# A re-annealed instruction order for an adaLN attention and GEGLU block on one core: refitted transfer model, loads moved by first use, clock-keeping matmuls redistributed

## The chip, the cores and the metric

The kernel runs on one core of one Trainium2 chip. The metric is the device time of one execution in microseconds (us), as timed from outside. The profile's span of the core is shorter by nearly a constant: the two differ by 1.7 to 1.9 us. A run more than 1.5% above the fastest of its kernel is called slow and left out of ratios.

Engines: PE is TensorE, DVE is VectorE, ACT is ScalarE, POOL is GpSimd, SP is SyncE, which here only issues DMAs. All large loads share one queue: queue q1 moved 28.56 of the 28.84 MB (part 3 of the page), and SP's timeline has the loads in the order of the program.

## The reference, cut to what matters

```python
mod = silu(c) @ w_mod                        # six vectors of 512: sa, ca, ga, sb, cb, gb
h = layernorm(x) * (1 + ca) + sa             # x is 2048 x 512, bf16
q, k, v = split(h @ wqkv)                    # 32 heads of 16
# each position looks at 8 earlier ones, two apart (dilated, local)
o = softmax(q . k[pos - 2*w] * scale) @ v[pos - 2*w]
x = x + ga * (o @ wo)
h = layernorm(x) * (1 + cb) + sb
x = x + gb * ((gelu(h @ w_gate) * (h @ w_up)) @ w_down)    # 512 -> 1792 -> 512
```

## The kernel before

The kernel cuts the 2048 rows into five groups (256, 256, 512, 512, 512) and pipelines them: QKV and the attention of one group run beside the feed-forward part (FFN) of the group before. It does not issue instructions as it goes. Every piece of work is recorded as an operation with an estimated duration; 948 of them are then emitted in the order that a list, `ORDER`, gives. That list came from an annealing search over a small time model, which is part of the kernel's source. The model decides one thing at build time too: how many clock-keeping matmuls (matmuls on zeros, whose result nobody reads) are put in front of a TensorE operation.

```python
ORDER = [0, 8, 52, 1, 6, 38, 28, 5, 29, 30, ...]      # 948 indices, cut

class Plan:
    LAND = 1.65
    SLOW = (4.0, 1.7)         # assumed in the model: the transfer pipe stands still for 1.7 us after 4.0 us
    # ...
    def emit(self):
        placed = self.order()
        pes, early = [o for o in placed if o.eng == "pe"], True
        for o, q in zip(pes, pes[1:]):
            early = early and o is not self.cold
            q.fill = int((q.at - o.at - o.us - 0.2) / 0.216) if early else 0
        # ... then emits each operation, with q.fill clock-keeping matmuls ahead of it
```

`self.cold` is one clock-keeping matmul that stands between the last transposes of the first group and its QKV; after it none is added. (The transposes of the second group, eight of them, may stand in between too.) These are the loads that the argument touches. They are numbered in the order in which they are recorded, not in which they are issued:

```python
load_x(0, 2, -1000)                                   # op 6: rows of the first group (x0)
load_cols(wm01, w_mod, 0, 2 * D, -999)                # op 7: sa, ca
first = [load_cols(wq, A_wqkv, 0, D, -998)]           # op 8: Q weights
load_x(2, 4, -997, first)                             # op 9: rows of the second group (x1)
load_cols(wkv, A_wqkv, D, 3 * D, -996)                # op 10: K and V weights
load_x(4, 8, -989, first)                             # op 11: rows of the third
# ...
for i in range(2):
    load_cols(Wg[i], B_w_gate, i * F // 2, (i + 1) * F // 2, -894 + 2 * i)
    load_cols(Wu[i], B_w_up, i * F // 2, (i + 1) * F // 2, -893 + 2 * i)
# ...
for i in range(2):                                    # the two halves of w_down
    lo, hi = i * FT // 2, (i + 1) * FT // 2
    dma(918e3, ..., out=WdP[:, lo:hi, :], ...)        # WdP0, WdP1
```

An FFN of the first group needs all of Wg and Wu; this kernel takes the second column halves (Wg1, Wu1) first, so the last gate and up weights to be loaded are Wg0 and Wu0. "The second half of Wu" in the prediction means the one loaded second, which is Wu0.

## Time and profile before

| what | where it is read | before |
|---|---|---|
| time, median of 3 runs (range) | timer | 254.38 us (253.68 to 254.77) |
| span of the profiled run | head of the page | 251.0 us |
| TensorE busy | page, part 1 | 240.7 us, 96% |
| half clock | clock record | 13.20 to 16.61 us |
| longest wait of TensorE | waits | 2.4 us, for Wu |
| clock-keeping matmuls, the first 14 of warm-up included | built program | 28 |

Part 1 of the page of the kernel before, with the span above it (busy time, share, number of instructions):

```profile
span 251.0 us, 4233 instructions
...
PE 240.7 (96%) x1624; PEld 126.4 (50%) x1642; DVE 165.9 (66%) x313; ACT 151.5 (60%) x278; POOL 18.0 (7%) x43
```

TensorE is busy nearly all the time, so a new order can only win the little that is not busy, and what runs at half clock. The waits of TensorE, before (what waited, for what: us in total, times, the longest):

```profile
PE u_ps L745 <- DMA Wu<-in_B_w_up_dram: 2.4, 1, 2.4
PE warm_ps L401 <- DVE neghalf L289: 1.3, 1, 1.3
PE tp L507 <- DVE xn L483: 1.0, 1, 1.0
...
PE g_ps L745 <- DMA Wg<-in_B_w_gate_dram: 0.3, 1, 0.3
```

The longest one is for a weight half that is in the queue behind others. SP's timeline, before, shows the order of issue (start, us to issue, line, what; the landing is elsewhere in the trace, Wu at 65.6 us):

```profile
52.53 0.64 SPq L391 DMA_DIRECT2D WdP<-in_B_w_down_dram  x1
...
56.61 0.60 SPq L365 DMA_DIRECT2D Wu<-in_B_w_up_dram  x1
...
57.93 0.60 SPq L391 DMA_DIRECT2D WdP<-in_B_w_down_dram  x1
```

So half of the down weights (0.9 MB) goes ahead of the up weights that TensorE will need first. The other place is the start. The windows view, before (stretch, its length, busy time and count of PE, PEld, DVE, ACT and POOL, then the share of full TensorE clock, the DMA share and GB/s):

```profile
7.00:12.00 5.00, 4.47 (x57) 2.49 (x55) 3.27 (x11) 0.96 (x5) 4.03 (x12) 1.00 1.06 386
12.00:16.00 4.00, 3.27 (x19) 2.42 (x21) 3.74 (x11) 2.71 (x7) 2.39 (x11) 0.65 1.08 317
...
60.00:75.00 15.00, 12.55 (x106) 7.59 (x105) 10.31 (x17) 9.89 (x18) 0.00 (x0) 1.00 1.11 254
```

TensorE's clock is halved over most of 12 to 16 us, when QKV of the first group starts; and in 60 to 75 us TensorE is busy for only 12.55 of 15 us, at full clock. No other stretch of the 250 us has as much to win.

### The profile page before, as it was taken

How to read it: one execution, taken by the hardware profiler on the slowest of the kernel's cores; microseconds unless marked ns; L12 is line 12 of the kernel's file. 1: busy time of each engine (PE TensorE's matmuls, PEld its weight loads, DVE VectorE, ACT ScalarE, POOL GpSimd, SP SyncE). 2: the span in 40 equal slices, each digit the busy share in tenths (PEclk: the TensorE clock that was granted, in tenths of full speed). 3: DMA queues.
4: the chain of work that ended last, by engine and by line, in shares of the span. 5: the costliest groups of instructions: out<-in, count | busy, mean ns of one | idle time of the engine just before them, and what ended most of it. 6: DMA issues, size and time to landing. Idle time of an engine off the chain costs nothing.

```text
span 251.0 us, 4233 instructions
## 1 busy us (share of the span) xinstructions
PE 240.7 (96%) x1624; PEld 126.4 (50%) x1642; DVE 165.9 (66%) x313; ACT 151.5 (60%) x278; POOL 18.0 (7%) x43
## 2 busy tenths in 40 slices
PE   7899999989699999999999999999999999999993
PEld 2489655556447575655444444444444444444441
DVE  1799999999578999879999555765345413122213
ACT  2258879689389955696463778506549821657300
POOL 1740220200001000010000010000001100000000
PEclk9979999999999999999999999999999999999999
DMA  6995999999994430554330006601000402000001
GB/s 178 376 310 149 212 274 264 275 296 334 278 204 112 89 83 1 138 123 104 109 64 0 3 19 129 129 24 61 0 3 0 84 0 81 6 0 0 0 24 63
DMA packets 36566, 28.84 MB, mean 115 GB/s; under 512 B 12865, under 2 KB 34626, under 8 KB 36546
## 3 DMA queue, kind: packets, MB, share of 16 engines
q1 hardware_dynamic: 36544, 28.56, 45.6%
q8 instruction: 13, 0.21, 0.4%
q14 instruction: 7, 0.06, 0.1%
q10 hardware_dynamic: 2, 0.00, 0.0%
HBM read 21.40 MB, written 4.28 MB: 102 GB/s over the span
## 4 chain that ended last, share of the span: by engine, by line
PE 87%; DMA 5%; DVE 3%; ACT 1%; issue 1%; POOL 1%; SPq 1%; POOLq 0%
PE y_ps L767 19%; PE u_ps L745 19%; PE g_ps L745 19%; PE qkv_ps L558 16%; PE x_ps L722 5%; DMA Wu<-in_B_w_up_dram 4%; PE o_ps L707 3%; PE LT L614 3%; DMA x_sg<-in_A_x_dram 2%; DVE st L473 1%; PE LT L645 1%; PE tp L507 1%; PE mb_ps L444 1%; PE rB L676 1%; ACT vT L563 1%
## 5 line engine op out<-in xcount | busy, mean ns | idle before, releaser
L745 PE MATMUL u_ps<-h2T,Wu 128*128 128x512 bf16 (+1 forms) x280 | 55.6, 337 | 2.4 <-DMA Wu<-in_B_w_up_dram 2.4
L745 PE MATMUL g_ps<-h2T,Wg 128*128 128x512 bf16 (+1 forms) x280 | 55.3, 337 | 0.3 <-DMA Wg<-in_B_w_gate_dram 0.3
L767 PE MATMUL y_ps<-WdP,hht 128*128 128x512 bf16 x217 | 49.5, 379 | 0.4
L756 ACT CAST ub<-u_ps 128x512 bf16<-128x512 f32 x56 | 32.3, 589 | 23.5 <-PE u_ps L745 22.8
L754 ACT ACTIVATE gl<-g_ps 128x512 bf16<-128x512 f32 x56 | 32.9, 601 | 21.5 <-PE g_ps L745 21.1
L757 DVE TENSOR_TENSOR hht<-gl,ub 128x512 bf16<-128x512 bf16 x56 | 23.0, 422 | 34.5 <-ACT gl L754 18.7
L745 PEld LDWEIGHTS <-Wu 128*128 128x128 bf16 x280 | 26.9, 98 | 25.8 <-DMA Wu<-in_B_w_up_dram 2.9
L745 PEld LDWEIGHTS <-Wg 128*128 128x128 bf16 x280 | 26.7, 98 | 24.3 <-issue 2.5
L767 PEld LDWEIGHTS <-hht 128*128 128x128 bf16 x224 | 21.7, 98 | 25.6
L558 PE MATMUL qkv_ps<-hT,wkv 128*128 128x512 bf16 (+1 forms) x157 | 31.2, 337 | 0.2
L598 DVE TENSOR_TENSOR pq<-qT,kT 128x2048 bf16<-128x2048 bf16 x24 | 28.1, 1219 | 0.1
L691 DVE TENSOR_TENSOR pv<-e,vR 128x2048 bf16<-128x2048 bf16 x24 | 28.0, 1218 | 0.1
L479 POOL TENSOR_TENSOR rstd<-rstd,neghalf 128x2 f32<-128x2 f32 x16 | 12.7, 794 | 176.2 <-DVE rstd L468 111.3
L774 DVE TENSOR_TENSOR ot<-y_ps,x_sg 128x512 bf16<-128x512 f32 x16 | 11.0, 691 | 20.9 <-PE y_ps L767 20.1
L558 PEld LDWEIGHTS <-wkv 128*128 128x128 bf16 x160 | 17.1, 114 | 8.4 <-issue 1.1
L558 PE MATMUL qkv_ps<-hT,wq 128*128 128x512 bf16 (+1 forms) x79 | 17.1, 362 | 0.1
L722 PE MATMUL x_ps<-woP,oT 128*128 128x512 bf16 x58 | 15.0, 379 | 0.3
L713 ACT CAST oT<-o_ps 128x512 bf16<-128x512 f32 x16 | 9.0, 592 | 9.8 <-PE o_ps L707 9.8
L473 DVE BATCH_NORM_STATS2 st<-x_sg 128x6 f32<-128x512 bf16 x16 | 10.8, 675 | 4.3 <-DMA x_sg<-in_A_x_dram 4.3
L495 ACT ACTIVATE h2T<-h2T,modT,scl 128x512 bf16<-128x512 bf16 (+1 forms) x16 | 11.0, 751 | 4.0 <-DMA h2T<-xn 4.0
L465 ACT ACTIVATE xn<-x_sg,xsum 128x512 bf16<-128x512 bf16 x16 | 11.5, 718 | 3.2 <-DVE xsum L462 3.0
L726 DVE SCALAR_TENSOR_TENSOR x_sg<-x_ps,x_sg 128x512 bf16<-128x512 f32 x16 | 10.7, 686 | 3.2 <-PE x_ps L722 3.2
(88 smaller groups left out, 214.0 us busy)
## 6 DMA issues: line engine op xcount, KB each, us to landing
vR<-scr SPq DMA_DIRECT2D x24, 260.0 KB, 4.5
vR<-scr SPq DMA_DIRECT2D x8, 264.0 KB, 6.9
wm<-in_w_mod_dram SPq DMA_DIRECT2D x4, 512.0 KB, 5.3
out_dram<-ot SPq DMA_DIRECT2D x16, 128.0 KB, 1.7
Wg<-in_B_w_gate_dram SPq DMA_DIRECT2D x2, 896.0 KB, 6.0
Wu<-in_B_w_up_dram SPq DMA_DIRECT2D x2, 896.0 KB, 9.4
WdP<-in_B_w_down_dram SPq DMA_DIRECT2D x2, 896.0 KB, 6.8
scr<-vT SPq DMA_DIRECT2D x6, 264.0 KB, 4.7
```

The costliest lines, as they stand in the source:

```text
L465: act(0.75, lambda i=i, xn=xn, nm=nm, mv=mv, c0=c0: nc.scalar.activation(out=xn[:, i, :], in_=x[g, c0 + i], func=ACT.Square, bias=nm[:, i: ...
L473: dve(0.59, lambda i=i, st=st, c0=c0: nc.vector.bn_stats(out=st[:, i, :], in_=x[g, c0 + i]), r=[x.key(g, c0 + i)], w=[(st, i)], pri=p)
L479: gp(0.65, lambda rstd=rstd: nc.gpsimd.tensor_tensor(out=rstd[:], in0=rstd[:], in1=neghalf[:, 0:2], op=ALU.pow), r=[rstd, neghalf], w=[rst ...
L558: nc.tensor.matmul(ps[:, j - j0, :], lhsT=(wkv[:, dt, (b - 1) * D + j:b * D:4] if b else wq[:, dt, j:D:4]), rhs=h_cols(hT, g, dt), start=( ...
L598: dve(1.14, lambda j=j, wg=wg, t=pq[m]: nc.vector.tensor_tensor(out=t[:], in0=_ap(q[g][:, j, 0:n], [[0, 4], [1, n]]), in1=_ap(k[g][:, j, : ...
L691: dve(1.14, lambda jj=jj, jl=jl, wg=wg, t=pv[m]: nc.vector.tensor_tensor(out=t[:], in0=_ap(e[:, wg, :], [[0, 4], [1, n]]), in1=vR[g][jj][: ...
L722: nc.tensor.matmul(x1_ps[:], lhsT=oT[:, j, c4 * P:(c4 + 1) * P], rhs=woP[:, j, :], start=(j == 0), stop=(j == 3))
L745: nc.tensor.matmul(ps[:, ft - f0, :], lhsT=Wt[ft // 7][:, dt, ft % 7 * P:(ft % 7 + 1) * P], rhs=h_cols(h2, g, dt), start=(dt == 0), stop=( ...
L754: act(0.485, lambda gl=gl, ps=gu[0]: nc.scalar.activation(out=gl[:], in_=ps[:], func=ACT.Gelu_apprx_tanh), r=[gu[0]], w=[gl], pri=p, table ...
L756: act(0.475, lambda ub=ub, ps=gu[1]: nc.scalar.copy(out=ub[:], in_=ps[:]), r=[gu[1]], w=[ub], pri=p)
L757: dve(0.335, lambda gl=gl, ub=ub, ht=ht: nc.vector.tensor_tensor(out=ht[:], in0=gl[:], in1=ub[:], op=ALU.mult), r=[gl, ub], w=[ht], pri=p)
L767: nc.tensor.matmul(y_ps[:], lhsT=hh[ft // nf][:, ft % nf, c4 * P:(c4 + 1) * P], rhs=WdP[:, ft, :], start=(ft == 0), stop=(ft == FT - 1))
```

## The change: intent and diff

The same arithmetic is emitted in another order. The order was annealed again over a model whose constants had been refitted: slower transfers, later landings, shorter VectorE operations in the softmax, up to about 1 us of extra slack (`late`) for weights. The clock-keeping rule was made slightly more generous, and the last one before QKV is asked to carry two more.

```diff
 ORDER = [
-    0, 8, 52, 1, 6, 38, 28, 5, 29, 30, 39, 36, 37, 40, 41, 43, 9, 130, 4, 42, 31, 7, 11, 33, 32, 44, 131, 34, 10, 35,
+    5, 52, 51, 0, 29, 28, 6, 36, 37, 9, 38, 128, 129, 1, 30, 39, 40, 41, 42, 43, 44, 47, 130, 131, 7, 132, 32, 31, 11,
     ... (948 indices, nearly all moved; cut)
-    SLOW = (4.0, 1.7)
+    SLOW = (4.0, 1.5)
     ... (model of drain latency on VectorE and TensorE; cut)
-            q.fill = int((q.at - o.at - o.us - 0.2) / 0.216) if early else 0
+            q.fill = max(q.warm, int((q.at - o.at - o.us - 0.1) / 0.216)) if early else 0
-        self.dma = lambda n, fn, bw=360e3, ring="sp", **kw: ...
+        self.dma = lambda n, fn, bw=350e3, ring="sp", **kw: ...
     def load_wm(b, p, after=()):
-            late=0.3 if b > 1 else 0.0)
+            bw=330e3, late=1.0)
-    first = [load_cols(wq, A_wqkv, 0, D, -998)]
+    load_cols(wq, A_wqkv, 0, D, -998)
-                pl.cold = pe(0.22, filler, r=[warm, tp], w=[wps], pri=-960)
+                pl.cold = pe(0.66, filler, r=[warm, tp, modT, scl], w=[wps], pri=-960)
+                pl.cold.warm = 2
-                    r=[scr], w=[(t, r)], pri=-985 if g == 0 else -950, bw=205e3, late=0.3)
+                    r=[scr], w=[(t, r)], pri=-985 if g == 0 else -950, bw=185e3, late=0.7)
```

What comes out, from building both: the clock-keeping matmuls fall from 28 (14 of warm-up, 13 ahead of the modulation columns, 1 among the transposes) to 17 (14 of warm-up, and 3 between the modulation columns and the second group's transposes, after which QKV starts). The loads at the start become x0, x1, wm01, x of the third group, wkv, wq, where they had been wq, x0, x1, wm01, x of the third group, wkv; QKV of the first group begins with K and V. Later, Wu0 is issued ahead of both halves of WdP instead of between them.

## The prediction

> **What bounds the kernel now.** TensorE. The page has it busy 240.7 of 251.0 us (96%), VectorE 165.9, ScalarE 151.5; the chain of waits is 87% TensorE. In the timeline I compared each matmul's start-to-start time with the pace of its shape (about 0.216 us for 512 columns). From 75 us to the last matmul at 247 us almost nothing is lost, so a new order gains nothing there. What can be won is small and early:
>
> 1. Start. The first QKV matmul starts at 13.73 us, after clock-keeping matmuls, modulation columns and transposes; the last transposes waited 1.04 us for xn.
> 2. Clock. The trace has TensorE at half clock for 3.4 us, from 13.2 to 16.6 us, just as QKV begins (windows view: 0.81 granted over 14 to 21 us, 1.00 later). That costs about 1.7 us.[...]
> 3. Weights. At 62.8 us TensorE waits 2.4 us[...] for the second half of Wu, whose load stands in the DMA queue behind half of WdP. It is TensorE's longest wait.
> 4. Two waits near 51 and 55 us (modulation columns, Wg), about 1 us together.
> 5. The tail, 247.0 to 251.0 us: output add 0.69 us, store 1.7 us. Unchanged.
>
> **What the change does.** No arithmetic changes; work is reordered. Building both: 28 clock-keeping matmuls become 17, so "more" holds only for the three (was one) just before QKV. That removes 11 x 0.216 us, but in time that waits for data: worth nothing by itself. Loads start with x, not wq, and wq comes after wkv; QKV of the first group starts with K and V. In the trace 3.67 MB stood up to the end of wkv, which landed at 14.3 us; now 3.15 MB, at about 0.36 MB/us: about 12.9 us (estimate). x lands at about 4.1 instead of 5.5 us, wm01 at 8.7 instead of 10.1, so LN and modulation are no longer last: QKV starts at 12.9 us, bound by wkv, 0.8 us sooner. V to scratch starts near 15.5 us instead of 21.25, closing the hole in DMA at 20 to 24 us. The second half of Wu is issued before both halves of WdP, 0.9 MB sooner, and lands before its use. Item 3 goes.
>
> **Sum.** Start -0.8, Wu -2.5, small waits -0.5; clock -1.7 with chance 0.35 only, because TensorE now idles 1 to 2 us before wkv lands, with 0.65 us of clock-keeping work in that window: -0.6 on average. New small stalls +0.4. Net -4.0 us: 250.4 us. All of it is on the critical path: TensorE is saturated from there to the end, so what is won before 70 us passes through.
>
> **Chances.** 250.4 us, range 248.6 to 252.4. Faster by over 2% (under 249.3): 0.27; within 2%: 0.71; slower: 0.02.
>
> **What the profile would show.** First QKV matmul at 12.5 to 13.2 us, released by the DMA of wkv; no TensorE wait over 0.5 us for Wu; the first logits fold at 21 to 23 us (24.86 now); last matmul to end still 3.9 us. A half-clock window of about 3.4 us still near 13 us in the likelier case; if gone, I am 1.2 us too high.
>
> **What would make it wrong.** wkv landing after 13.5 us[...]; two half-clock windows instead of one; vR gathers ahead of hT transposes starving QKV of group 3 near 45 to 60 us; Wu still late because the queue is blocked behind a gather that waits for VectorE.

The sum came to -4.0 us (-0.8 - 2.5 - 0.5 - 0.6 + 0.4), from 254.38 to 250.4 us. The rate of 0.36 MB/us agrees with the windows view of the kernel before (355 GB/s from 3 to 14 us). The 1.7 us of the clock term are half of the 3.41 us at half clock in that trace; its chance of 0.35, and that idling ahead of QKV brings the half clock, were the author's estimate, which e3, e4 and e9 test.

## More of the kernel before

The down weights are scaled by `gb` in place on VectorE, in seven pieces of two slices:

```python
for f0 in range(0, FT, 2):
    dve(0.6, ... out=WdP[:, f0:f0 + 2, :], in0=WdP[:, f0:f0 + 2, :], in1=gbB ...)   # ops 79 to 85
```

Slices 0 to 6 come with the load WdP0, slices 7 to 13 with WdP1.

## The result, and the profile after

Ratios are the mean time of one kernel's fast runs over that of the other kernel's fast runs of the same rounds, so they are not quite the ratio of the medians quoted. The kernel after took **250.62 us (median of 4, 250.25 to 251.22)** against 254.06 us (253.68 to 254.77) for the one before in the same rounds: ratio **0.9864, 95% interval 0.983 to 0.9897**, so within 2%. The profiled spans are 251.0 and 248.5 us, a difference of 2.5 us, against 3.4 us for the medians; the point "Medians and spans" near the end comes back to that.

Part 1 of the page, after:

```profile
span 248.5 us, 4223 instructions
...
PE 237.8 (96%) x1613; PEld 125.0 (50%) x1631; DVE 166.1 (67%) x313; ACT 153.3 (62%) x278; POOL 18.6 (7%) x43
```

The waits of TensorE, after. The wait for Wu is gone and none over 0.8 us is left on weights; the 2.1 us at the top lies in the warm-up, where nothing is lost by it:

```profile
PE c_ps L422 <- DMA crow<-in_c_dram: 2.1, 1, 2.1
PE tp L515 <- DVE xn L491: 1.7, 2, 1.1
PE modT_ps L437 <- DMA wm<-in_w_mod_dram: 0.8, 1, 0.8
PE mb_ps L452 <- DMA wm<-in_w_mod_dram: 0.4, 1, 0.4
PE qkv_ps L567 <- DMA wkv<-in_A_wqkv_dram: 0.3, 1, 0.3
```

SP's timeline, after. Wu is issued 4.4 us sooner, before both halves of WdP; it landed at 58.8 us and was first used at 59.67:

```profile
52.26 0.64 SPq L373 DMA_DIRECT2D Wu<-in_B_w_up_dram  x1
53.00 1.37 SPq L579 DMA_DIRECT2D scr<-vT  x2
54.41 1.53 SPq L399 DMA_DIRECT2D WdP<-in_B_w_down_dram  x2
```

The windows view, after:

```profile
7.00:12.00 5.00, 2.55 (x43) 1.53 (x43) 3.57 (x10) 1.35 (x4) 3.00 (x11) 1.00 1.02 362
12.00:16.00 4.00, 3.24 (x20) 2.37 (x21) 3.61 (x13) 2.21 (x5) 1.60 (x4) 0.57 1.11 352
...
60.00:75.00 15.00, 14.72 (x117) 8.13 (x116) 13.38 (x24) 13.30 (x25) 0.00 (x0) 1.00 1.05 234
```

In 60 to 75 us TensorE is busy 2.17 us longer than before, and that is most of the 2.5 us of the spans. At the start the clock is halved as long as before (12.40 to 15.82 us). The start itself did not move. TensorE's timeline, before, at the first QKV matmuls (start, us, what, how many):

```profile
13.73 3.32 PE L558 MATMUL qkv_ps<-hT,wq 128*128 128x256 bf16 x16
```

and after:

```profile
13.79 2.89 PE L567 MATMUL qkv_ps<-hT,wkv 128*128 128x256 bf16 x16 [0.35 <-DMA wkv<-in_A_wqkv_dram]
```

13.79 against 13.73 us, where 12.9 had been predicted. The trace has sixteen completions for this load, one for each share of it. They came at 11.34 (first), 11.96 (median) and 13.74 us (last), and the first matmul that reads wkv started 0.05 us after the last. The estimate of 12.9 was made from bytes over a rate; the median share was 0.9 us ahead of it, the last 0.8 us behind. The bytes themselves weren't late: added up packet by packet, SP's queue had moved 3.15 MB by 11.88 us, and the first share of wq, the next load, landed at 12.84, before the last one of wkv. The median is not steady: in the six other profiles with the same loads up to wkv (e2, e3, e4, e8, e9, e11) it lies between 12.1 and 13.3 us, the last share between 13.3 and 13.9. In the kernel before, the spread of the same load is 13.23 to 14.31 us. Other loads spread as well: wm01, after, from 6.85 to 9.21 us.

From the first QKV on the two kernels go level until the weights: the logits fold starts 1.24 us sooner (23.62 against 24.86), but after has by then done eight fewer QKV matmuls of 256 columns, which are worth 0.87 us. The last matmul starts at 244.32 against 246.80 us, and both need some 4 us from there to the end. So the gain is made between about 50 and 75 us, and nearly all of it is kept.

### The profile page after: what moved, and what is told of

Same layout as the page of the kernel before. It is cut to its first block, busy times and chain, and to the rows that moved or that the text cites. A ratio compares the mean times of both kernels' runs of the same rounds, so it can differ in the third digit from the quotient of the medians.

```text
span 248.5 us, 4223 instructions
## 1 busy us (share of the span) xinstructions
PE 237.8 (96%) x1613; PEld 125.0 (50%) x1631; DVE 166.1 (67%) x313; ACT 153.3 (62%) x278; POOL 18.6 (7%) x43
## 4 chain that ended last, share of the span: by engine, by line
PE 84%; DMA 9%; ACT 3%; SPq 1%; DVE 1%; issue 1%; POOL 1%; POOLq 0%; ACTq 0%
PE u_ps L756 19%; PE y_ps L778 19%; PE g_ps L756 19%; PE qkv_ps L567 12%; PE x_ps L733 5%; DMA wkv<-in_A_wqkv_dram 4%; PE LT L625 3%; PE o_ps L718 3%; DMA hT<-xn 2%; DMA wm<-in_w_mod_dram 2%; ACT hT L503 1%; PE LT L656 1%; PE mb_ps L452 1%; POOL rstd L487 1%; DVE xn L491 1%
## 5 line engine op out<-in xcount | busy, mean ns | idle before, releaser
L768 DVE TENSOR_TENSOR hht<-gl,ub 128x512 bf16<-128x512 bf16 x56 | 22.5, 422 | 30.7 <-ACT gl L765 21.0
L567 PE MATMUL qkv_ps<-hT,wkv 128*128 128x512 bf16 (+1 forms) x158 | 32.9, 346 | 0.7 <-DMA wkv<-in_A_wqkv_dram 0.3
L567 PE MATMUL qkv_ps<-hT,wq 128*128 128x512 bf16 (+1 forms) x79 | 16.5, 337 | 0.1
L574 ACT CAST kT<-qkv_ps 128x512 bf16<-128x512 f32 x16 | 9.2, 586 | 3.7 <-PE qkv_ps L567 3.2
```

The costliest lines, as they stand in the source:

```text
L567: nc.tensor.matmul(ps[:, j - j0, :], lhsT=(wkv[:, dt, (b - 1) * D + j:b * D:4] if b else wq[:, dt, j:D:4]), rhs=h_cols(hT, g, dt), start=( ...
L768: dve(0.335, lambda gl=gl, ub=ub, ht=ht: nc.vector.tensor_tensor(out=ht[:], in0=gl[:], in1=ub[:], op=ALU.mult), r=[gl, ub], w=[ht], pri=p)
```

## The experiments

The texts quoted below use letters as working names of theories; the sentences ahead of each say in words which theories were at stake. All runs used five rounds. e1 to e4 went together on one chip, as did e5, e6, e8 and e9, then e7, e10 and e11; e12 went alone. The runs of before are shared within a batch. All twelve gave the right result.

### Is it the place of the Wu load? e1 and e2

The first theory: the wait for Wu is the gain, so exchanging two loads in the kernel before should bring most of it, and moving WdP1 ahead of Wu0 in the kernel after should take it away. The rival: the time up to 75 us in the kernel before is set by all the weights that have yet to arrive, so the wait only moves to the next of them.

e1, in the kernel before:

```diff
 ORDER (kernel before)
-  ... 456, 123, 26, 216, ...      # WdP1 here
-  ... 183, 20, 450, ...           # Wu0 here
+  ... 456, 123, 20, 216, ...
+  ... 183, 26, 450, ...
```

> The kernel before, with one edit: in the DMA queue the second load of Wu and the first load of WdP change places. Theory A (most of the gain is the Wu wait): TensorE's 2.4 us wait for Wu near 63 us is gone, the span falls by 2.0 to 2.7 us from 251.0, ratio to before about 0.990. Rival B (the gain comes from the rest of the new order; the wait only moves, to a later wait on the scaled WdP or on a PSUM buffer): the Wu wait goes but the span falls by under 1 us, ratio 0.996 or more.

Measured: 254.81 us (252.45 to 257.58) against 254.78; ratio 0.9971 (0.9913 to 1.0028). No gain that can be told from zero. The profiled run of e1 was slow (span 254.7 us), so its waits serve to show where, not how long in total. The waits of TensorE in e1:

```profile
PE g_ps L745 <- DMA Wg<-in_B_w_gate_dram: 2.8, 1, 2.8
PE LT L645 <- DVE m L640: 2.2, 1, 2.2
```

The wait for Wu is gone. In its place TensorE waits for Wg, earlier, and for the softmax maximum, later. VectorE's timeline tells why the maximum is late. Before:

```profile
71.17 1.29 DVE L792 TENSOR_TENSOR WdP<-WdP,gbB 128x1024 bf16<-128x1024 bf16 x2 [1.73 <-DMA WdP<-in_B_w_down_dram]
72.38 0.42 DVE L636 TENSOR_TENSOR Lb<-Lb 128x512 bf16<-128x512 bf16 x1
```

and e1:

```profile
73.31 1.29 DVE L792 TENSOR_TENSOR WdP<-WdP,gbB 128x1024 bf16<-128x1024 bf16 x2 [4.00 <-DMA WdP<-in_B_w_down_dram]
74.52 0.42 DVE L636 TENSOR_TENSOR Lb<-Lb 128x512 bf16<-128x512 bf16 x1
```

The order has two scalings of WdP in front of the maximum, and the first needs WdP0, the last weight load of all. VectorE kept to the order of the program: in e1 it idled for 4.00 us ahead of the first scaling and began the first step of the maximum (L636) directly behind both, at 74.52 us; in the kernel before, ScalarE had cast `Lb`, the input of that step, by 71.38 us, and there too it began only behind the scalings, at 72.38. So the softmax of the third group stands behind a DMA. In the kernel before this was hidden, because TensorE had been held up by Wu anyway. The rival was right for the load alone: **the wait moved.** One part of this profile may be chance. Wg0 stands ahead of both exchanged loads, so the exchange doesn't explain why it is late here. TensorE's wait for it was 0.3 us in the profile of before, 0.5 in e5, 0.7 in e6, 0.9 in e7, 2.8 in e1 and 3.0 in e12; why it varies is open.

e2, in the kernel after:

```diff
 ORDER (kernel after)
-  ... 182, 20, 184, ...  313, 216, 316, 26, 314, ...
+  ... 182, 26, 20, 184, ...  313, 216, 316, 314, ...
```

> The kernel after, with one edit: the first load of WdP is put ahead of the second load of Wu. In the trace of after that Wu lands at 58.8 us and is first used at 59.7, so 0.9 MB ahead of it at about 0.36 MB/us makes it about 1.6 us too late. Theory A: a TensorE wait for Wu of 1.3 to 2.0 us returns and the span is 249.8 to 250.6 us against 248.5. Rival B (slack elsewhere absorbs it): span within 0.5 us of 248.5.

Measured: 255.27 us (254.36 to 257.05) against 254.78; ratio 1.0035 (0.999 to 1.0081). The whole gain is lost, and more than 1.3 to 2.0 us: the span is 253.2 us, 4.7 above that of the kernel after. TensorE's timeline of e2 shows the reason:

```profile
63.08 1.13 PE L756 MATMUL u_ps<-h2T,Wu 128*128 128x256 bf16 x8 [3.03 <-DMA Wu<-in_B_w_up_dram]
64.00 1.91 PE L567 MATMUL qkv_ps<-hT,wkv 128*128 128x512 bf16 x4
```

The wait is back at 3.03 us, and the four matmuls after it take 1.91 us where four of the same shape took 1.03 us a few us earlier: the clock is halved from 63.92 to 67.33 us. Here the wait of 3.03 us cost itself and then a half-clock window of 3.41 us, which is up to 1.7 us. The place of Wu is thus necessary for the gain in the new order (e2); alone in the old order it gave no gain clear of noise (e1).

### Loads and scalings together: e6 and e7

If the scalings in front of the maximum are the second half of the cause, e1 with the scalings moved must bring the gain. e6 moves five of them behind the softmax:

```diff
 ORDER (e1), operations 79, 80, 82, 83, 84 scale WdP
-  ... 25, 80, 318, 83, ... 185, 84, 204, ... 190, 79, 325, ... 442, 82, 195, ...
+  ... 330, 80, 83, 300, 334, 332, 84, 79, 331, 333, 82, 306, ...     # after e, between the products with V
```

> The kernel before with the two loads exchanged as in e1_before_wu_first, and also VectorE's five scalings of WdP moved behind the softmax maximum, so that nothing TensorE needs soon waits for WdP. Theory A' (in e1 the gain was lost because VectorE then waited for WdP in front of the maximum that TensorE needs): now neither the wait for Wu nor the one for the maximum shows, TensorE's waits between 55 and 80 us fall under 1 us together, span 248 to 249.3 if the clock has one half window, ratio 0.985 to 0.992. Rival (the DMA is late as a whole, any order waits somewhere): a wait of over 1.5 us shows up at another place before 90 us, ratio 0.995 or more.

Measured: 253.07 us (252.06 to 257.41) against 253.55; ratio 0.9978 (0.9947 to 1.001), well under what was hoped. The wait for Wu is gone and that for the maximum is 0.3 us, but the waits of TensorE show a new one:

```profile
PE o_ps L707 <- DVE pv L691: 2.0, 3, 1.1
...
PE g_ps L745 <- DMA Wg<-in_B_w_gate_dram: 0.7, 1, 0.7
```

The scalings (about 0.6 us each) now stand between the products with V, on which TensorE depends, while VectorE had idled for about 5 us between 65 and 79 us. The place was badly chosen. e7 puts the same five one by one into idle time of VectorE:

```diff
 ORDER (e1), operations 79, 80, 82, 83, 84 scale WdP
-  ... 25, 80, 318, 83, ... 185, 84, 204, ... 190, 79, 325, ... 442, 82, 195, ...
+  ... 322, 83, 203, ... 189, 84, 323, ... 205, 80, 191, ... 442, 79, 195, ... 332, 82, 331, ...
```

> The kernel before with the two loads exchanged, and VectorE's five scalings of WdP placed in the idle places that VectorE has between 66 and 80 us: those that need the half of WdP that lands first go first, the rest later, one of them between the products with V. Theory A'' (in e1 the wait moved to VectorE's WdP scaling and in e6 to VectorE's products with V, both because of where the scalings stand): now TensorE's waits for Wu, for the maximum and for the products are together under 1.5 us, ratio to before 0.989 to 0.995. Rival (what Wu gives back is lost again elsewhere, wherever the scalings stand): waits of over 2 us in sum between 60 and 95 us, ratio 0.997 or more.

Measured: 251.60 us (250.95 to 252.61) against 254.39; ratio 0.9912 (0.9863 to 0.9961). That is the same ratio as the kernel after showed when run again (e8, below: 0.9911). The waits of TensorE in e7:

```profile
PE g_ps L745 <- DMA Wg<-in_B_w_gate_dram: 0.9, 1, 0.9
PE o_ps L707 <- DVE pv L691: 0.5, 1, 0.5
```

So an exchange of two loads and a new place for five VectorE operations, out of 948, bring the ratio to that of the change in one of its two batches. They don't bring all of it, for the two had different luck with the clock: the six runs of the kernel after with one half-clock window have spans of 248.5 to 249.3 us, the four of e7 with one have 249.8 to 250.8, some 1.5 us more by the means; e7 drew level because its other two runs had none, where four of the other kernel's ten had two. What makes up this rest isn't shown. The load order alone gave no gain clear of noise, with the scalings late little, with the scalings in idle time 0.9%. The intervals of e1, e6 and e7 overlap and the three ran in three batches. That the scalings are the other half of the cause rests on the traces (the wait for the maximum, 2.2 us in e1, isn't among e7's waits) more than on the times.

### Do the clock-keeping matmuls matter? e3, e4 and e8

Two theories on the two extra clock-keepers: they are too few to matter, since the clock is halved near 13 us with and without them; or they shorten the half-clock stretch. e4 leaves one instead of three. e3 adds eight to the kernel after: five more in the same place and three between the second group's transposes and QKV.

```diff
 e4, kernel after
             q.fill = max(q.warm, int((q.at - o.at - o.us - 0.1) / 0.216)) if early else 0
+            q.fill = 0 if q is self.cold else q.fill
```

> The kernel after, with one clock-keeping matmul before the second group's transposes instead of three, as before had. Theory D' (the two extra do nothing, since the clock halves in spite of them): same span within 0.4 us, the half-clock window stays at one of 3.4 us. Rival (they shorten or move the half-clock window): span up by 0.5 us or more, or a second half-clock window.

Measured: 252.33 us (251.23 to 253.05) against 254.78; ratio 0.9913 (0.9873 to 0.9953). By time alone that can't be told from the kernel after (0.9864 in one batch, 0.9911 in another, e8). The clock tells more: all six runs of e4 have a mean granted clock of 0.986, which is two windows at half clock (a window of 3.413 us at half clock loses 1.7065 us; (1 - 0.986) of some 250 us is 3.5 us, or 2.05 times that). Of the ten runs of the kernel after, six have one window and four have two. The windows view of e4:

```profile
12.00:16.00 4.00, 3.31 (x21) 2.30 (x22) 3.28 (x11) 2.52 (x5) 1.90 (x6) 0.55 1.11 349
16.00:20.00 4.00, 4.00 (x24) 2.96 (x22) 2.30 (x5) 1.29 (x3) 1.71 (x8) 0.60 0.75 183
```

In this run the clock stays at half from 12.40 to 19.23 us, against 12.40 to 15.82 in the kernel after. So the theory that two matmuls do not matter fell, by the counts: none of six runs with a single window against six of ten, which chance alone would give about once in 40. That evidence is across batches, and how they act isn't shown by the one profile: they run ahead of 12.40 us, and the clock drops at 12.40 in both.

```diff
 e3, kernel after
-            q.fill = max(q.warm, ...) if early else 0
+            q.fill = max(q.warm, ...) if early else q.warm
-                pl.cold.warm = 2
+                pl.cold.warm = 7
+    pl.ops[59].warm = 3        # ahead of the first QKV
     pl.emit()
```

> The kernel after, with 8 more clock-keeping matmuls in the time in which TensorE waits before QKV: 8 instead of 3 before the second group's transposes, and 3 between them and the first QKV matmul. Theory C (the half clock from 12.4 us comes from too little TensorE work in the window before it): the half-clock window near 12.4 us is gone, QKV's first 16 matmuls take about 1.9 us instead of 2.9, span lower by 0.7 to 1.2 us. Rival D (the two extra clock-keeping matmuls do nothing, and neither do eight[...]): the half-clock window stays, span within 0.4 us of 248.5 or above by the time the matmuls delay.

Measured: 250.16 us (248.18 to 251.87) against 254.78; ratio 0.9831 (0.9774 to 0.9887). The profiled run has no half clock at all. The windows view of e3:

```profile
7.00:12.00 5.00, 3.54 (x49) 2.01 (x48) 3.79 (x10) 1.33 (x4) 3.01 (x11) 1.00 1.04 368
12.00:16.00 4.00, 4.00 (x37) 3.20 (x36) 3.47 (x12) 2.97 (x7) 1.68 (x4) 1.00 1.09 359
```

and its first QKV matmuls in the timeline:

```profile
13.54 1.94 PE L567 MATMUL qkv_ps<-hT,wkv 128*128 128x256 bf16 x16
```

The same sixteen matmuls took 2.89 us in the kernel after and take 1.94 here. The six runs of e3 fall into two kinds: three without a half-clock window, with spans of 246.4 to 247.3 us, and three with one, 249.4 to 250.1: further apart than the 1.7 us of the clock alone.

e8 is the kernel after once more, in another batch, to see how much it scatters.

> The kernel after, unchanged, beside the others on this chip: ratio to before 0.983 to 0.990, about one half-clock window in most runs (clock 0.992 to 0.993), where before has two in most (0.986).

Measured: 251.25 us (250.29 to 251.97) against 253.55; ratio 0.9911 (0.9883 to 0.994). Three of its runs have one half-clock window (spans 248.5, 248.5 and 249.3 us) and three have two (249.7 to 250.2). In the first batch of the kernel after three runs had one (248.5 to 249.1) and one had two (249.4, clock 0.986). **Most of this kernel's scatter is the number of half-clock windows**, which the source does not fix. The kernel before had 0 to 3 windows per run in the later batches, e2 up to four (clock 0.971 in its slowest run). By the clock one more window costs up to 1.7 us, 0.7% of 250 us, so for changes of 1% the windows must be counted run by run.

### Does a better start pay in the kernel before? e5

"What is won before 70 us passes through", said the prediction. The rival: in the kernel before the weights decide when 75 us is passed, so an earlier start only lengthens the waits for them. e5 gives the kernel before five clock-keepers ahead of QKV.

```diff
 e5, kernel before
-  ... 132, 47, 133, 45, ... 141, 48, 49, ...
+  ... 132, 47, 48, 133, 45, ... 141, 49, ...
             q.fill = int((q.at - o.at - o.us - 0.2) / 0.216) if early else 0
+            q.fill = 5 if q is self.cold else q.fill
```

> The kernel before with only clock-keeping matmuls added: 6 instead of 1 before QKV, put where TensorE waits for the second group's xn (11.5 to 12.6 us). Theory C (too little TensorE work in the window before QKV halves the clock; each half-clock window of 3.4 us costs up to 1.7 us): the half-clock window at 13 us is gone in the profile, the run falls by 1.0 to 1.7 us, ratio to before 0.993 to 0.996; the wait for Wu near 63 us stays. Rival (clock-keeping matmuls only help together with the new order): the window stays, ratio 0.998 to 1.002.

Measured: 254.49 us (252.34 to 254.61) against 253.55; ratio 1.0028 (0.9995 to 1.006). The half-clock window at the start is gone, and nothing is won. TensorE's timeline, e5:

```profile
61.80 1.05 PE L615 MATMUL LT<-pq,Mph 128*32 128x512 bf16 x16
65.81 2.47 PE L746 MATMUL u_ps<-h2T,Wu 128*128 128x256 bf16 x16 [2.96 <-DMA Wu<-in_B_w_up_dram]
```

and the same place before:

```profile
62.17 1.05 PE L614 MATMUL LT<-pq,Mph 128*32 128x512 bf16 x16
65.61 1.92 PE L745 MATMUL u_ps<-h2T,Wu 128*128 128x256 bf16 x16 [2.39 <-DMA Wu<-in_B_w_up_dram]
```

TensorE begins the fold in front of the wait 0.37 us sooner and waits 0.57 us longer, because Wu lands when it lands; and the longer wait brings a half-clock window of its own (67.03 to 70.44 us), seen in the 2.47 us of the sixteen matmuls. The rival was right for the end of the way, but that is not all: set beside each other by TensorE's weight loads, e5 leads before by 1.55 us at 18 us, by 0.65 at 33 to 46 and by 0.37 at 57 to 62. Most of the early gain was thus gone before the wait for Wu; new waits for VectorE's `pq` and `m` (0.2 and 0.3 us) are a part of that, the rest isn't explained. In the kernel after, where no FFN weight is waited for, the same kind of gain does pass through: by the same count e3 leads by 1.21 us at 18 us, 0.95 at 36 to 60 and 1.34 from 62 us to the end.

### A version that beats both: e9 and e11

e9 is e3 with four more clock-keepers ahead of the first modulation columns and with the two modulation rows exchanged, `ga` (whose weights land first) before `gb`, against the small wait for w_mod near 35 us.

```diff
 e9, e3 and
-  ... 24, 156, 76, 77, 164, 14, 278, 279, 15, 70, 71, 296, ...
+  ... 24, 156, 70, 71, 164, 14, 278, 279, 15, 76, 77, 296, ...
+    pl.ops[32].warm = 4
```

> A version meant to beat both: after with e3's 8 more clock-keeping matmuls, 4 more in the wait for the modulation weights (8.2 to 9.4 us), and the two modulation rows exchanged on TensorE and ScalarE, so that the row whose weights land at 35 us comes second. Theory C: no half-clock window at the start in most runs, the 0.4 to 0.6 us wait for modulation weights near 35 us gone; span 246 to 247, ratio to after about 0.99, to before 0.974 to 0.981. Rival: as e3_more_keep in three of its six runs, a half window comes elsewhere and the gain over after is under 0.5 us.

Measured: 249.00 us (248.33 to 249.74) against 253.55; ratio 0.9825 (0.9797 to 0.9852), 2.25 us under the kernel after in the same batch. Five of six runs have no half-clock window, the sixth a fraction of one (0.29), too short for a window (see the reading of the clock below). e11 repeats it:

> e9_keep_and_rows unchanged, beside e10 on this chip: ratio to before 0.979 to 0.985, no half-clock window in nearly all runs.

Measured: 249.41 us (249.03 to 250.37) against 254.39; ratio 0.9826 (0.9785 to 0.9868); again five of six runs without a half-clock window. It beats both kernels, by mean, in both batches.

### Can the start itself come sooner? e10

The theory: by bytes, wkv lands sooner if it is issued ahead of the half megabyte of x that is not needed yet. The rival: the landing of the last share does not follow the bytes, and VectorE would starve for those rows.

```diff
 e10, e9 and
-  ... 7, 132, 32, 31, 11, 133, 135, ...  256, 257, 260, 137, 10, 138, ...
+  ... 7, 132, 32, 31, 10, 11, 133, 135, ...  256, 257, 260, 137, 138, ...
   (and the statistics of those x rows moved later on VectorE; 3 and 2 clock-keepers instead of 7 and 3)
```

> e9_keep_and_rows with the wkv load put ahead of the load of rows 512 to 1023 of x, and the statistics of those rows moved back on VectorE so that it doesn't wait for them before the work for QKV. Theory E (QKV's start is set by the bytes in the queue up to wkv: 2.62 instead of 3.15 MB, at about 0.37 MB/us 1.4 us less): first QKV matmul at 12.2 to 12.8 us instead of 13.9. If TensorE is the only limit from there on, the span falls by about 1.2 us against e9 (ratio to it 0.995). Rival F (from 14 to 60 us VectorE is as full as TensorE, and it waits for these rows of x instead): QKV starts sooner but TensorE waits for pq or xn between 16 and 30 us, and the span is within 0.5 us of e9's or above.

Measured: 251.61 us (251.26 to 253.6) against 254.39; ratio 0.992 (0.9873 to 0.9967), 2.2 us worse than e11 in the same batch. First QKV and what followed, e10 (TensorE's and VectorE's timelines):

```profile
14.23 3.01 PE L567 MATMUL qkv_ps<-hT,wkv 128*128 128x256 bf16 x16
...
25.35 0.84 PE L625 MATMUL LT<-pq,Mph 128*32 128x256 bf16 x24 [0.74 <-DVE pq L615]
```

```profile
14.60 1.29 DVE L481 BATCH_NORM_STATS2 st<-x_sg 128x6 f32<-128x512 bf16 x2 [1.56 <-DMA x_sg<-in_A_x_dram]
```

With 0.52 MB fewer ahead of it, wkv's last share landed at 13.07 us, 0.8 us before that of e11 (13.85), where the bytes had promised 1.4. But wm01 landed later (10.36 instead of 9.71 us). The modulation columns waited for it, and behind them in TensorE's order the transposes and two clock-keepers, at half clock from 13.07 us, ran until QKV began at 14.23. VectorE waited for the rows that had been put back. So the landing followed the bytes in part, QKV didn't follow the landing, and on the time the rival was right. Four of its six runs have no half-clock window at all, at spans of 249.5 to 251.7 us, where e11's have 247.3 to 247.8, so the clock isn't the reason.

### The early gain on top of e7: e12

e12 joins e7 and e5: with the weights no longer waited for, e5's gain at the start ought to pass through in the old order too. The rival: it is lost at the next weight.

```diff
 e12, e7 and the two edits of e5
```

> The kernel before with the edits of e7_wu_first_scale_split and the five clock-keeping matmuls of e5_before_keep together. Theory G (the clock-keeping matmuls gained nothing in e5 because TensorE then only came sooner to the wait for Wu; with that wait gone what is won at the start passes through): the half-clock window near 13 us is gone, span 247.8 to 249.0, ratio to before 0.983 to 0.988, that is 0.4 to 0.7% under e7's 0.991, though e5 alone was at 1.003. Rival (the start is not critical for another reason, such as VectorE): ratio 0.990 to 0.993, as e7, and TensorE waits grow elsewhere by what was won.

Measured: 251.48 us (250.55 to 254.29, 8 runs) against 254.20; ratio 0.9888 (0.9844 to 0.9933), which the interval doesn't separate from e7's 0.9912. The waits of TensorE in the profiled run of e12:

```profile
PE g_ps L746 <- DMA Wg<-in_B_w_gate_dram: 3.0, 1, 3.0
```

That profiled run is the slowest of the eight (span 252.6 us): 3.0 us lost to Wg, and a half-clock window directly after. Runs without a half-clock window have spans of 249.1 to 249.8 us, the same as e7's two (249.2 and 249.3). So here too the early gain mostly did not arrive. By weight loads, the profiled e12 leads that of e7 by 1.73 us at 18 us and by 0.8 from 34 to 55, and then runs into Wg. This stays inconclusive: there is one profile, and none of the seven faster runs.

## A reading of the clock: what halves it and what brings it back

Every half-clock stretch between the warm-up and the last matmuls is one or two windows of 3.41 us long. (The clock drops once more at the end, at 247.92 us in the kernel after; where that falls inside the span, it gives a run a fraction of a window.) For ten of these windows the table has TensorE's busy time in the 3.41 us directly ahead of the drop, or inside the half-clock window itself. The records give the first half-clock stretch as 3,413 ns in the kernel before and in the kernel after. The places fit the same length: in each of the 14 traces every recorded change of the clock lies a whole number of windows after the first one, to within 1 ns (in the kernel before, 72 windows of 3,413.3 ns from 6.370 to 252.129 us). (Busy time is as the profile models it, so the figures are rough.)

| window | TensorE busy in it, of 3.41 us | clock of the next window |
|---|---|---|
| before, 9.79 to 13.20 | 2.25 | half |
| e1, 9.22 to 12.63 | 2.02 | half |
| e2, 9.31 to 12.72 | 1.98 | half |
| after, 8.99 to 12.40 | 1.68 | half |
| e2, 60.51 to 63.92 | 0.84 | half |
| e4, 12.40 to 15.82 (half) | 2.73 | half again |
| e8, 12.12 to 15.53 (half) | 2.65 | half again |
| e2, 12.72 to 16.13 (half) | 2.92 | full |
| after, 12.40 to 15.82 (half) | 3.06 | full |
| before, 13.20 to 16.61 (half) | 3.31 | full |

No window had to be idle for the clock to drop: it dropped after up to 2.25 us busy of 3.41. The longest single wait of TensorE was 1.04 us in the window from 9.79 us (before) and 1.14 us in that from 8.99 us (after). But busy time alone doesn't decide it. In e1 the window from 53.59 to 57.00 us had 1.71 us busy, in the kernel before the one from 64.40 to 67.81 had 2.2, and both were followed by full clock. Of the half-clock windows seen, those with up to 2.73 us busy were followed by another and those with 2.92 or more by full clock.

The work in a window sorts them better than the time. Count the columns of the moving operand (512 for a 128x512 matmul, 1 for a modulation column; a matmul across an edge shared by time). Of 1009 windows in the 14 traces, the 20 that were followed by half clock had up to 3,230 columns, and the 989 that were followed by full clock had 3,369 or more, but for one with 3,146 (e11). That holds at half and at full clock: e4's and e8's half-clock windows with 3,123 and 2,863 columns brought another, e2's and after's with 3,379 and 3,369 didn't. So the limit in these traces lies somewhere between 3,100 and 3,400 columns per window (an estimate from this count). It would also explain why the start is in danger: the 32 modulation columns keep TensorE busy for about 1 us (0.95 in the kernel before) and add 32 columns. This is a count over the traces; no run was made to test it. Which side a run falls on depends on where the window lies: in e4 the second group's transposes ran at 11.95 us, ahead of it, and in e8 the window ended 0.3 us sooner than in the first profile of the same program. e3 and e9 stay at full clock. Their first recorded change (to full clock, at 6.03 and 6.12 us) places their windows: in those from 9.45 to 12.86 (e3) and 9.54 to 12.95 us (e9) TensorE was busy for 3.16 and 2.99 us, where the kernel after had 1.68 in its own from 8.99 to 12.40.

## Why the prediction was right or wrong, point by point

- **Total.** 250.4 us predicted (248.6 to 252.4), 250.62 measured, class within 2%. It was right, but the sum behind it was not: one term was absent and the others came out smaller or went by another way.
- **"Start -0.8".** Wrong: 13.79 against 13.73 us. The step that failed is "3.67 MB ... now 3.15 MB, at about 0.36 MB/us: about 12.9 us". The median share came at 11.96 us; the last one came at 13.74. The 3.15 MB had moved by 11.88 us, so the rate wasn't too high; what failed is that the bytes moved in the whole queue tell when the last share of one load lands. The prediction named the risk of a landing after 13.5 us, for another reason, which was not shown. Why the last shares lag is open, and so is why the rate sags to 238 and 258 GB/s between 4 and 6 us (346 the microsecond before, 360 after; in the kernel before 241 in each of 5 to 6 and 6 to 7 us, between 371 and 381). The trace doesn't tell which DMA engine a late share belongs to. In e10 half a megabyte fewer ahead of wkv brought its landing 0.8 us sooner, not 1.4, and QKV no sooner.
- **"Wu -2.5".** Right in size for the change, wrong as a cause. The wait of 2.4 us went, and 2.17 us more of TensorE work lie in 60 to 75 us. But in e1 the load order alone brought nothing clear of noise; the place of the scalings on VectorE, which the prediction did not mention, is the other half. e7, with both, reaches the ratio of one batch of the change, though at the same number of half-clock windows it is still some 1.5 us behind.
- **"Small waits -0.5".** Not shown. Wg's 0.3 us went, but waits for w_mod (0.8 and 0.4 us) came.
- **Clock.** "Still near 13 us in the likelier case": right, 12.40 to 15.82. But "worth nothing by itself" was too low an opinion of these matmuls: with one instead of three, six runs of six had a second half-clock window, which six of ten runs of the kernel after had not; eight more (e3) get rid of the last window in half the runs, twelve more (e9, e11) in ten of twelve. The 13 that the change took away ahead of the modulation columns may have been missed too, since e9 put four of them back and is the steadiest, but no run takes those alone.
- **"TensorE is saturated from there to the end, so what is won before 70 us passes through."** False for the kernel before, where of 1.55 us won early 0.37 was left at 62 us, and that became 0.57 us more of waiting (e5) and a half-clock window. It held for the kernel after (e3), where no FFN weight is waited for. The sentence should have been tested on the wait at 65 us: if the wait's end is a DMA, an earlier arrival only lengthens it.
- **The first logits fold at 21 to 23 us.** 23.62: missed by 0.6 us, as the start did not move. V to scratch began at 19.13 instead of the 15.5 predicted (21.25 before).
- **Medians and spans.** The medians differ by 3.4 us, the spans by 2.5 us, and e8's batch by 2.3 us. The number of half-clock windows per run differs from batch to batch; three of four runs of the kernel after had a single window in the first, three of six in e8's. The profiled run of the kernel before took 252.71 us by the timer, 1.7 us less than the median of three (254.38) from which the prediction counted. The predicted gain of 4.0 us is above all three differences, so its closeness to 250.62 is partly luck.
- **Open.** How the parts of the gain add up exactly (e1, e6, e7 and e12 are not additive), what the change has over e7 at equal clock, why Wg's landing varies, why the load rate sags at 4 to 6 us, and whether e12's early gain is lost to Wg in its fast runs.

## What to carry to other kernels

If a wait ends with a DMA, removing another wait ahead of it or starting earlier may buy nothing, as in e5: look at what lands last and who stands behind it, in the DMA queue and also on an engine that keeps to the program's order, as VectorE did here (4.00 us idle ahead of a scaling in e1), where a small operation that needs the last load can hold up a softmax that doesn't. Move the load and that operation together, and put the operation in idle time of its engine, or the wait only changes its name. And when TensorE must wait near the start, give it clock-keeping work until the real matmuls come, and go by the columns in a window rather than by busy time (a count above, not a test): twelve matmuls on zeros, about 2.6 us of them in time that was idle anyway, were worth 2.25 us here together with the exchange of two small rows, and only repeated runs with the granted clock beside each show it.
